# Loads and scalings of units 5 to 9 moved earlier in the first two groups of a fused attention and feed-forward kernel

## The chip, the cores and the metric

The kernel runs on one core of a Trainium2 chip. The metric is the device time of one execution in microseconds (us). A core has a matrix engine (TensorE, PE in the profile; its weight loads are PEld), a vector engine (VectorE, DVE), a scalar engine (ScalarE, ACT), GpSimd (POOL) and SyncE (SP). SyncE here only issues DMAs; GpSimd issues those of the weights and of v, and computes as well.

## The reference

Two stages: linear attention with decay over 4 batches, 8 heads, 768 positions and head size 64, and a bilinear feed-forward layer over the 3072 resulting rows of 512.

```python
for b in range(nb):                      # blocks of positions
    intra = (q_b @ k_b.T * Dmask) @ v_b  # Dmask: lam**(i-j) for i >= j, else 0
    inter = (q_b * lam_pow) @ kv_state
    out[b] = intra + inter
    kv_state = lam_block * kv_state + (k_b * rev_pow).T @ v_b
x = out as 3072 rows of 512
y = ((x @ w_a) * (x @ w_b)) @ w_out      # w_a, w_b: 512 x 1536, w_out: 1536 x 512
```

## The kernel before, in words

The 3072 rows are 24 units of 128 rows (6 to a batch). `GROUPS = (4, 2, 4, 4, 4, 4, 2)` cuts them into feed-forward groups: units 0 to 3, then 4 and 5 (group 1), then 6 to 9 (group 2), and so on. While the feed-forward layer of one group runs, the attention of the next group's units is put between its matmuls.

Per unit, in `prep_k` (L263, step "P" of the plan): k is scaled by a power of lam on VectorE for units 4 to 9 and on GpSimd from 10 on (`make_ks`, L249; the instruction is at L244), q is scaled on GpSimd (`make_qs`), from unit 6 on a transposing DMA is issued on SyncE (L269), then `pump` issues more loads of q and k, and outside it `make_vb` (L257) loads v by a DMA that GpSimd issues. Units 4 and 5 are transposed on TensorE instead (step "T", L275). Step "S" computes the scores of a unit (L294) and masks them (two VectorE instructions, L311). Step "V" updates the state by matmuls (L358) and copies it out on VectorE (L391). Step "O2" takes two units, computes their attention output (L328), copies it to `xT` on ScalarE (L351), and, with the last unit of a group, makes the four sums of x (`sums`, L480 to L483) that the group's products need.

`pump` (L160) walks a list `pending`. An entry ("q", u) or ("k", u) issues a 256 KB load on SyncE's queue, into one of four buffers each for q and k (`load_x`, L123), unless u is 3 or more ahead of the units already prepared; then it stops until the next step P. An entry "after" is a gate: a copy of one element out of a weight tile, which SyncE can issue only once that part of the weights has landed; all later loads stand behind it. In order the list before has: gate on part 3 of w_b, unit 4, gate on part 0 of w_out, unit 5, gate on part 3 of w_out, unit 6, gate on part 5 of w_out, unit 7 and on. The first call of `pump` is just ahead of group 0.

`PLAN` (L43) gives for each group pairs of a slot and a step; `hook(slot)` emits the steps of a slot between matmuls. Group 0 (`ffn`, L621) has slots 0 to 11 after the feed-forward products and 12 to 35, each after two output matmuls (L612). Groups 1 to 6 use `ffn_seven` (L488), a product with seven instead of eight block products. `step(i, n)` is product n of column block i, called (i, n) below. For group 1, i is 0 to 2, and the products run in the order

```
(0,1) (0,5) (0,2) (0,6) (0,3) (1,1) (0,7) (1,5) (1,2) (1,6) (0,4) (1,3) (2,1) (1,7) (2,5) (2,2) (2,6) (1,4) (2,3) (2,7)
```

with the slots of `hook` after (0,1): 0, (0,6): 1, (0,7): 2, (1,6): 3, (1,7): 4, (2,6): 5, (2,7): 6 and 7, and then 11; then come eight output matmuls, the last product (2,4), and the slots from 12 on.

Each product is eight matmuls (L502) into one of seven PSUM banks that are handed out in turn. ScalarE copies three of a block's partial results out (L517). VectorE then forms c11 (product 2, L536), c12 (product 3, L547), c22 (product 7, L553) and the second half of `ab` (product 4, L556), and GpSimd the first half (L549). Product 4 adds to the bank that c22 reads. `SUM_ON_VEC` (L42) lists the blocks whose c11 is made on VectorE; for the others ScalarE makes one more copy and GpSimd adds (L539).

The pool `wst` has 13 buffers of 4 KB per partition, used by the first loads of q and k (six of them, free once units 0 to 3 are scaled), the weight sums, the x sums, `s12` and kept outputs.

Of the kernel before, what the change touches and what calls it, by code (L numbers as in the profile page):

```python
# [16 lines left out]
F32 = mybir.dt.float32  # L17
# [5 lines left out]
def _bc(ap, dims):  # L23
# [15 lines left out]


S_GROUPS = (1, 2, 3, 4, 5, 6)
SUM_ON_VEC = {1: (0, 1, 2), 2: (0, 1, 2, 3, 5), 3: (1, 3, 5), 4: (1, 3, 5), 5: (1, 2, 4, 5), 6: (0, 1, 2)}  # L42
PLAN = {  # L43
    0: [(0, "V", 3), (1, "TW", 0), (3, "TW", 1), (5, "TW", 2), (7, "TW", 3), (11, "TW", 4),
        (15, "P", 4), (18, "TW", 5), (19, "T", 4), (20, "P", 5), (22, "S", 4), (25, "T", 5), (26, "V", 4),
        (27, "P", 6), (28, "S", 5), (31, "O2", (4, 5)), (33, "P", 7)],
    1: [(2, "P", 8), (4, "P", 9), (6, "S", 6), (7, "V", 6), (7, "S", 7), (11, "O2", (6, 7)),
        (12, "S", 8), (12, "V", 8), (13, "S", 9), (13, "P", 10), (14, "O2", (8, 9)), (15, "P", 11)],
    2: [(1, "P", 12), (4, "P", 13), (7, "P", 14), (11, "S", 10), (11, "S", 11), (12, "P", 15),
        (14, "P", 16), (17, "P", 17)],  # L50
# [11 lines left out]
def kernel(  # L62
# [11 lines left out]
    nc = tc.nc  # L74
    B, H, S, D = q.shape
# [5 lines left out]
    NU = B * NB  # L81
# [6 lines left out]
    wst_pool = ctx.enter_context(tc.tile_pool(name="wst", bufs=13))  # L88
    ld_pool = ctx.enter_context(tc.tile_pool(name="ld", bufs=4))
# [31 lines left out]
    raw = {}  # L121

    def load_x(w, u):  # L123
        b, nb = divmod(u, NB)
        t = ld_pool.tile([128, H, D], F32, name=w + "f", tag=w + "f", bufs=4)
        nc.sync.dma_start(out=t, in_={"q": qr, "k": kr}[w][b, nb])
        raw[u, w] = t

    wa_sb = singles.tile([128, KS, d_ff], BF16, name="wa_sb")
    wb_sb = singles.tile([128, KS, d_ff], BF16, name="wb_sb")  # L130
    wo_sb = singles.tile([128, FC, d_model], BF16, name="wo_sb")
# [4 lines left out]
    w_off = [sum(W_CHUNKS[:i]) for i in range(len(W_CHUNKS) + 1)]  # L136
# [7 lines left out]
    def load_w(kind, c):  # L144
        if kind == "o":
            nc.gpsimd.dma_start(out=wo_sb[:, 2 * c:2 * c + 2, :], in_=wo_r[:, 2 * c:2 * c + 2, :])
        else:
# [1 line left out]
                                in_=w_part(wa_r if kind == "a" else wb_r, c))  # L149

    n0 = GROUPS[0]
    pending = [("after", ("b", 3)), ("q", n0), ("k", n0), ("after", ("o", 0)), ("q", n0 + 1), ("k", n0 + 1),
               ("after", ("o", 3)), ("q", n0 + 2), ("k", n0 + 2), ("after", ("o", 5))]
    for u in range(n0 + 3, NU):
        pending += [("q", u), ("k", u)]
    landed = singles.tile([1, 16], BF16, name="landed")
    q_here = singles.tile([128, 1], F32, name="q_here")
    used = {"u": 0, "gates": 0}

    def pump():  # L160
        while pending:
            kind, c = pending[0]
            if kind == "after":
                i = used["gates"] = used["gates"] + 1
                nc.sync.dma_start(out=landed[:, i:i + 1],
                                  in_=wo_sb[0:1, 2 * c[1] + 1, 0:1] if c[0] == "o" else
                                  wb_sb[0:1, 3, w_off[c[1]]:w_off[c[1]] + 1])
            elif c >= used["u"] + 3:
                return
            else:  # L170
                load_x(kind, c)
            pending.pop(0)
# [15 lines left out]
    for w, src in (("q", q), ("k", k)):  # L188
# [3 lines left out]
        for c in range(0, HP, n_c):  # L192
            t = wst_pool.tile([128, 1024], F32, name=w + "4", tag="wst")[:, :n_c * 512]
            t = t.rearrange("p (c b x) -> p c b x", c=n_c, b=2)
# [68 lines left out]
    def prep_k(u):  # L263
        make_ks(u, "dve" if u < n0 + 6 else "pool")
        make_qs(u, "pool")
        used["u"] = u + 1
        if u in DMA_T:
            qkT = qkT_pool.tile([128, 2, HP, 128], BF16, name="qkT", tag="qkT")
            nc.sync.dma_start_transpose(  # L269
                out=qkT[:].rearrange("p j hp i -> p (j hp) i"),  # L270
                in_=U[u]["qk"][:].rearrange("p j h d -> p (j h d)"))
            U[u]["qT"], U[u]["kT"] = qkT[:, 0], qkT[:, 1]
        pump()
# [214 lines left out]
    def ffn_seven(g, u0, n, xT, hook, last):  # L488
# [31 lines left out]
        def step(i, n):  # L520
# [10 lines left out]
            elif n == 2:  # L531
                p, pb = bank_of("m_p")
                product(i, p, w_of(wa_sb, 2, i), x12, True)
                d["c11"] = a_pool.tile([128, nf, h], BF16, name="c11", tag="a")
                if i in SUM_ON_VEC[g]:
                    nc.vector.tensor_add(d["c11"], d["s12"][:, 0], p)  # L536
# [254 lines left out]
    bank["held"].clear()  # L791
    used["u"] = n0
    pump()

    for g, n in enumerate(GROUPS):
# [62 lines left out]
```

## Time and profile before

| | |
|---|---|
| four runs | 225.86 to 227.85 us, median 226.77 |
| the profiled execution | 226.27 us; span from first to last instruction 224.6 us |
| TensorE busy | 214.8 us, 96% of the span; granted clock 0.991 on average |
| VectorE, ScalarE, GpSimd busy | 148.8, 100.2, 121.0 us |
| DMA queue of SyncE (q1) | 23.53 MB, 47.3% of 16 engines' span |
| DMA queue of GpSimd (q0) | 7.87 MB, 38.4% |
| loads of q and of k, 20 each | 256 KB, median 4.7 and 5.5 us from issue to landing |

Times inside the execution are counted from its first instruction. Group 0's feed-forward products begin at 17.45 us and its output matmuls at 38.41. Group 1 begins at 52.86, its last output matmuls end near 76.9, where group 2 begins. "Busy" of TensorE includes time in which it runs at a lower clock. A wait is named by the instruction that waited and the one that released it; the chain of waits follows the execution back from its end through those releases.

### The profile page before, as it was taken

The numbers are of one execution on the slowest core, as the hardware profiler recorded it, in microseconds if no ns is written. First come the engines' busy times: TensorE is split into PE (matmuls) and PEld (weight loads), VectorE is DVE, ScalarE is ACT, GpSimd is POOL, SyncE is SP. The second block draws the span as 40 slices with busy tenths as digits, with TensorE's granted clock in tenths as the row PEclk, the third lists the DMA queues.
The fourth block names the chain that finished last, engine by engine and source line by source line (L and its number), as shares of the span: only waits on it lengthen the run. The fifth ranks groups of instructions, "written<-read, shape, count | busy, mean of one in ns | idle before, by whom it ended". The sixth has DMA issues, their size and how long they took to land.

```text
span 224.6 us, 5362 instructions
## 1 busy us (share of the span) xinstructions
PE 214.8 (96%) x2171; PEld 148.2 (66%) x2171; DVE 148.8 (66%) x254; ACT 100.2 (45%) x179; POOL 121.0 (54%) x134
## 2 busy tenths in 40 slices
PE   7799999989959999999999999999999999999994
PEld 2476444447935688855588855688854688745973
DVE  0992995674994789793877773678873687820760
ACT  2685232118601565523366523566423556333622
POOL 6879541160898339997059994069920146400230
PEclk9999999999997999999999999999999999999999
DMA  4999999999999995999985959509511200012102
GB/s 125 299 182 193 204 197 181 195 219 165 208 217 186 240 175 71 234 332 228 207 227 66 169 146 231 141 0 74 70 50 47 93 4 0 0 50 93 50 3 93
DMA packets 98608, 31.81 MB, mean 142 GB/s; under 512 B 86552, under 2 KB 95640, under 8 KB 98584
## 3 DMA queue, kind: packets, MB, share of 16 engines
q1 hardware_dynamic: 66392, 23.53, 47.3%
q0 software_dynamic: 31904, 7.87, 38.4%
q8 instruction: 17, 0.28, 0.5%
q10 hardware_dynamic: 288, 0.07, 0.1%
q14 instruction: 7, 0.06, 0.1%
HBM read 28.32 MB, written 6.29 MB: 154 GB/s over the span
## 4 chain that ended last, share of the span: by engine, by line
PE 73%; DMA 13%; DVE 4%; POOL 3%; ACT 2%; SPq 2%; issue 1%; ACTq 0%
PE op L612 24%; PE m_q L502 23%; PE m_r L502 12%; PE m_p L502 6%; DMA kf<-in_k_dram 6%; DMA wo_sb<-in_moe_w_out_dram 5%; PE o_ps L328 4%; DMA k<-in_k_dram 3%; PE kq L294 2%; DVE m L311 2%; POOL wa_sb L148 1%; POOL wb_sb L148 1%; SPq L196 1%; PE kvd L358 1%; ACT o_kept L603 1%
## 5 line engine op out<-in xcount | busy, mean ns | idle before, releaser
L612 PE MATMUL op<-wo_sb,ab 128*128 128x512 bf16 (+2 forms) x312 | 69.0, 367 | 0.0
L549 POOL TENSOR_TENSOR ab<-c,c 128x512 bf16<-128x512 bf16 x30 | 34.8, 1164 | 43.2 <-DVE c L547 42.3
L502 PEld LDWEIGHTS <-tw 128*128 128x128 bf16 x576 | 49.1, 98 | 6.4 <-issue 0.3
L612 PEld LDWEIGHTS <-ab 128*128 128x128 bf16 x312 | 28.0, 99 | 27.4 <-issue 1.1
L502 PE MATMUL m_q<-xs,tw 128*128 128x256 bf16 (+1 forms) x288 | 36.1, 255 | 0.2 <-ACT s L517 0.2
L311 DVE TENSOR_TENSOR m<-kq,lotri 128x512 bf16<-128x512 f32 x47 | 29.8, 683 | 4.2 <-PE kq L294 3.8
L607 ACT COPY o_sb<-op 128x512 f32<-128x512 f32 (+2 forms) x20 | 10.9, 543 | 43.5 <-PE op L612 43.5
L556 DVE TENSOR_TENSOR ab<-c,m_q 128x512 bf16<-128x512 f32 x30 | 20.6, 687 | 13.0 <-PE m_q L502 11.2
L244 POOL TENSOR_TENSOR qk<-qf,lp_q 128x512 bf16<-128x512 f32 x20 | 21.8, 1089 | 13.3 <-DMA qf<-in_q_dram 13.3
L539 POOL TENSOR_TENSOR c<-s 128x512 bf16<-128x512 f32 x9 | 11.5, 1274 | 30.8 <-ACT s L517 30.7
L502 PEld LDWEIGHTS <-wa_sb 128*128 128x128 bf16 x288 | 24.5, 98 | 3.1
L517 ACT COPY s<-m_q 128x512 f32<-128x512 f32 x30 | 17.6, 588 | 15.0 <-PE m_q L502 14.9
L547 DVE TENSOR_TENSOR c<-u,m_r 128x512 f32<-128x512 f32 x30 | 20.4, 681 | 5.5 <-ACT u L517 5.5
L260 POOL DMA_DIRECT2D vb<-in_v_dram x24 | 22.4, 935 | 1.4 <-DMA wb_sb<-in_moe_w_b_dram 1.4
L536 DVE TENSOR_TENSOR c<-s,m_p 128x512 bf16<-128x512 f32 x21 | 14.4, 686 | 12.6 <-PE m_p L502 11.2
L553 DVE TENSOR_TENSOR c<-s,m_q 128x512 f32<-128x512 f32 x30 | 20.5, 685 | 0.5
L517 ACT COPY s<-m_r 128x512 f32<-128x512 f32 x30 | 17.7, 590 | 7.1 <-PE m_r L502 7.1
L517 ACT COPY u<-m_q 128x512 f32<-128x512 f32 x30 | 17.8, 593 | 5.9 <-PE m_q L502 5.9
L351 ACT CAST xT<-o_ps 128x512 bf16<-128x512 f32 x22 | 12.0, 588 | 17.4 <-PE o_ps L328 17.2
L502 PE MATMUL m_q<-xT,wa_sb 128*128 128x256 bf16 (+1 forms) x144 | 18.1, 255 | 0.0
L502 PE MATMUL m_q<-xT,tw 128*128 128x256 bf16 (+1 forms) x144 | 18.1, 255 | 0.0
L502 PE MATMUL m_r<-xs,tw 128*128 128x256 bf16 (+1 forms) x144 | 18.1, 255 | 0.0
(81 smaller groups left out, 264.2 us busy)
## 6 DMA issues: line engine op xcount, KB each, us to landing
qf<-in_q_dram SPq DMA_DIRECT2D x20, 256.0 KB, 4.7
kf<-in_k_dram SPq DMA_DIRECT2D x20, 256.0 KB, 5.5
out_dram<-o_sb SPq DMA_DIRECT2D x17, 256.0 KB, 2.0
vb<-in_v_dram POOLq DMA_DIRECT2D x24, 128.0 KB, 4.6
wa_sb<-in_moe_w_a_dram POOLq DMA_DIRECT2D x6, 256.0 KB, 6.2
wb_sb<-in_moe_w_b_dram POOLq DMA_DIRECT2D x6, 256.0 KB, 7.5
wo_sb<-in_moe_w_out_dram POOLq DMA_DIRECT2D x6, 256.0 KB, 12.1
out_dram<-o_kept SPq DMA_DIRECT2D x6, 256.0 KB, 3.5
```

The source lines that it names most:

```text
L244: eng_of(eng).tensor_mul(dst.rearrange("p (c b) d -> p b c d", b=2), x[:].rearrange("p (b c) d -> p b c d", b=2), lp.rearrange("p (b c) o ...
L260: nc.gpsimd.dma_start(out=vb, in_=vr[b, nb])
L311: nc.vector.tensor_mul(m, kq[i], lotri_bc)
L351: nc.scalar.copy(dst, src)
L502: nc.tensor.matmul(ps[:, f, :], lhsT=w(k, f), rhs=x[:, k, :], start=(first and f == 0 and k == 0), stop=True, skip_group_check=True)
L517: nc.scalar.copy(t, ps)
L536: nc.vector.tensor_add(d["c11"], d["s12"][:, 0], p)
L547: nc.vector.tensor_add(c12, d["u2"], d["r"])
L549: nc.gpsimd.tensor_mul(ab[:, nf * i:nf * i + nf, 0:h], d["c11"], c12)
L553: nc.vector.tensor_add(d["c22"], d["s5"], d["q"])
L556: nc.vector.tensor_mul(ab[:, nf * i:nf * i + nf, h:2 * h], d["c22"], d["q"])
L612: nc.tensor.matmul(op[:, lo:hi], lhsT=ab[:, f, t * 128:(t + 1) * 128], rhs=wo_sb[:, f, lo:hi], start=(f == 0), stop=(f == FC - 1))
```

## The change

Three things change.

- The list `pending` has two gates instead of four: on part 3 of w_b ahead of unit 4 (as before) and on part 5 of w_b ahead of unit 6. The bound on how far loads may run ahead is raised at the start, so that the first call of `pump` issues q and k of units 4 to 9.
- q and k of units 8 and 9 go into halves of one `wst` tile per unit instead of the four buffers, which units 4 to 7 hold.
- The plan: in group 0, T of unit 5 goes from slot 25 to 24, V of 4 from 26 to 25, S of 5 from 28 to 27, P of 6 from 27 to 28 (so behind S of 5), P of 7 from 33 to 30 (ahead of O2 of 4 and 5 with the x sums), and P of 8 from group 1 into slot 35 (behind O2). In group 1, P of 9 goes from slot 4 to 0, S of 6 from 6 to 4, V of 6 from 7 to 5 and S of 7 from 7 to 6. In group 1, c11 of block 1 is made by ScalarE and GpSimd instead of VectorE.

```diff
-SUM_ON_VEC = {1: (0, 1, 2), 2: (0, 1, 2, 3, 5), 3: (1, 3, 5), 4: (1, 3, 5), 5: (1, 2, 4, 5), 6: (0, 1, 2)}
+SUM_ON_VEC = {1: (0, 2), 2: (0, 1, 2, 3, 5), 3: (1, 3, 5), 4: (1, 3, 5), 5: (1, 2, 4, 5), 6: (0, 1, 2)}
 PLAN = {
     0: [(0, "V", 3), (1, "TW", 0), (3, "TW", 1), (5, "TW", 2), (7, "TW", 3), (11, "TW", 4),
-        (15, "P", 4), (18, "TW", 5), (19, "T", 4), (20, "P", 5), (22, "S", 4), (25, "T", 5), (26, "V", 4),
-        (27, "P", 6), (28, "S", 5), (31, "O2", (4, 5)), (33, "P", 7)],
-    1: [(2, "P", 8), (4, "P", 9), (6, "S", 6), (7, "V", 6), (7, "S", 7), (11, "O2", (6, 7)),
+        (15, "P", 4), (18, "TW", 5), (19, "T", 4), (20, "P", 5), (22, "S", 4), (24, "T", 5), (25, "V", 4),
+        (27, "S", 5), (28, "P", 6), (30, "P", 7), (31, "O2", (4, 5)), (35, "P", 8)],
+    1: [(0, "P", 9), (4, "S", 6), (5, "V", 6), (6, "S", 7), (11, "O2", (6, 7)),
         (12, "S", 8), (12, "V", 8), (13, "S", 9), (13, "P", 10), (14, "O2", (8, 9)), (15, "P", 11)],
...
     def load_x(w, u):
         b, nb = divmod(u, NB)
-        t = ld_pool.tile([128, H, D], F32, name=w + "f", tag=w + "f", bufs=4)
+        if u in (n0 + 4, n0 + 5):
+            if (u, "kq") not in raw:
+                raw[u, "kq"] = wst_pool.tile([128, 2, H, D], F32, name="qkf", tag="wst")
+            t = raw[u, "kq"][:, "qk".index(w)]
+        else:
+            t = ld_pool.tile([128, H, D], F32, name=w + "f", tag=w + "f", bufs=4)
         nc.sync.dma_start(out=t, in_={"q": qr, "k": kr}[w][b, nb])
...
     n0 = GROUPS[0]
-    pending = [("after", ("b", 3)), ("q", n0), ("k", n0), ("after", ("o", 0)), ("q", n0 + 1), ("k", n0 + 1),
-               ("after", ("o", 3)), ("q", n0 + 2), ("k", n0 + 2), ("after", ("o", 5))]
-    for u in range(n0 + 3, NU):
+    pending = [("after", 3)]
+    for u in range(n0, NU):
+        if u == n0 + 2:
+            pending.append(("after", 5))
         pending += [("q", u), ("k", u)]
...
-    used = {"u": 0, "gates": 0}
+    used = {"u": 0}
...
             if kind == "after":
-                i = used["gates"] = used["gates"] + 1
-                nc.sync.dma_start(out=landed[:, i:i + 1],
-                                  in_=wo_sb[0:1, 2 * c[1] + 1, 0:1] if c[0] == "o" else
-                                  wb_sb[0:1, 3, w_off[c[1]]:w_off[c[1]] + 1])
-            elif c >= used["u"] + 3:
+                nc.sync.dma_start(out=landed[:, c:c + 1], in_=wb_sb[0:1, 3, w_off[c]:w_off[c] + 1])
+            elif c >= max(used["u"] + 3, n0 + 6):
                 return
```

## The prediction

> **What bounds the kernel now.** I read the page first: TensorE is busy 96% of the span, so the change can earn only what TensorE loses. The waits of TensorE say where that is:
>
> ```profile
> PE o_ps L328 <- DVE st L391: 2.0, 1, 2.0
> ...
> PE tps L280 <- DVE qk L244: 0.9, 1, 0.9
> PE kq L294 <- DVE ab L556: 0.6, 1, 0.6
> ...
> PE m_q L502 <- ACT s L517: 0.2, 1, 0.2
> ```
>
> (Columns: waiting line, who ended the wait, us in all, times, longest.) Three of them end on VectorE, and all lie between 45 and 67 us. The chain of waits in that stretch:
>
> ```profile
> 33.16 12.70 DMA kf<-in_k_dram
> 45.86 0.02 issue
> 45.88 0.70 DVE qk L244
> 46.59 0.05 issue
> 46.63 0.40 PE tps L280 x4
> ...
> 62.45 0.68 DVE ab L556
> 63.12 0.06 DVE c L547
> 63.18 0.46 issue
> 63.64 0.68 DVE c L553
> 64.32 1.20 DVE m L311 x2
> 65.52 0.60 DVE st L391
> 66.11 0.61 DVE m L311
> 66.72 0.04 issue
> 66.77 1.02 PE o_ps L328 x12
> 67.79 0.21 PE kvd L380 x8
> 68.00 2.90 PE op L612 x8
> ```
>
> The reader should see two places. At 46 us TensorE waits for k of unit 5 to land and be scaled. From 62.45 to 66.72 the chain lies on VectorE: it is behind, and the masks and the state of units 6 and 7 come last. Then eight 512-column matmuls take 2.90 us; elsewhere in the chain two take 0.43, so eight should be 1.73. The stretch by half microseconds says why (columns: PE, PEld, DVE, ACT, POOL busy, granted clock, DMA share, GB/s):
>
> ```profile
> 64.50:65.00 0.50, 0.00 (x0) 0.00 (x0) 0.50 (x2) 0.00 (x0) 0.50 (x2) 1.00 1.26 283
> 65.00:65.50 0.50, 0.00 (x0) 0.00 (x0) 0.50 (x2) 0.00 (x0) 0.50 (x1) 1.00 1.27 265
> ...
> 66.50:67.00 0.50, 0.44 (x10) 0.33 (x12) 0.50 (x2) 0.00 (x0) 0.50 (x2) 0.73 1.42 228
> 67.00:67.50 0.50, 0.50 (x12) 0.35 (x9) 0.31 (x1) 0.28 (x1) 0.50 (x1) 0.50 1.36 163
> ...
> 69.50:70.00 0.50, 0.50 (x2) 0.15 (x1) 0.00 (x0) 0.00 (x0) 0.50 (x2) 0.50 1.46 244
> ```
>
> After the idle stretch the granted clock halves from about 66.7 to 70.1. From the last product of group 1 (ends 62.4) to 70.9 TensorE does about 3.6 us of work in 8.5: some 4.9 us are lost here, 1.7 of them to the clock. After that no wait over 0.2 us is listed, so what is won here stays won.
>
> VectorE is behind because it scales k of units 7, 8 and 9 at 53.05 (0.69 us), 57.22 (1.11) and 60.65 (1.28), while it stood idle 1.91 us before 52.12, 0.83 before 54.57 and 0.59 before 55.85. That is what the moved steps address.
>
> **The change, part by part.**
>
> *Gates and issue order.* Two of four gate copies go (0.60 and 0.88 us on SyncE; at 44.21 one delays q of unit 7), and k, q of unit 5 are issued at about 27.5 instead of 32.73 and 33.16. Does k of unit 5 land earlier? I counted the SyncE queue's 256-byte packets in the trace; q or k of one unit is 1,024. From 29 to 43 us they flow without a gap, one for one with those of the weights and v (161 against 161 in the microsecond from 31, 373 against 379 from 34). The queue is in order and already full, so issuing earlier buys nothing before packet 4,096 (k of unit 5), at 44.1. I take zero; if it does come earlier, at most the 0.91 us wait goes. SyncE itself stands in such issues (2.94 us at 33.16, 3.41 at 40.70, each until an older load has landed), so by the same pace it gets past k of 9 at about 50.4; the transposing DMA of 6, whose k is scaled at 50.8, finds it free.
>
> *Step T of unit 5 one slot earlier.* Its second half still waits until 46.63, but two matmuls that ran before the wait now run behind it: +0.43 us. Their cover is that wait, and it is lost. P, S and V of units 4 and 5 shift inside the same absolute times. Group 1 starts 0.43 later, at 53.29.
>
> *Units 6 and 7.* Step P issues, in order: k scaling on VectorE, q scaling on GpSimd (1.03), a transposing DMA on SyncE, two loads if some come free (now only from P of unit 7 on, as units up to 9 are issued), and v on GpSimd (0.94). k of 6 and 7 are now scaled behind the masks of unit 5 at about 50.1 and 50.7 and before the sums L480 to L483, in the 1.91 us that VectorE stood idle. k of 7 is complete at packet 8,192; before, that was at 49.0, and with the time from last packet to use of k of 5 (44.1 to 45.88, 1.8) it is usable at 50.8. Cover: the sums cannot start before ScalarE's copy ends at about 52.5, so 1 us of lateness is free; more delays group 1 one for one.
>
> *Units 8 and 9.* Their scalings come between the sums and the first product sums of group 1, and k of 9 stands ahead of c11 of product block 0 (L536), so whatever that load is late VectorE is late. This is the new wait. Behind it queue c11, c12, c22, and TensorE's product (0,4) at 57.75 + 0.43 = 58.2 overwrites the bank that c22 reads. When does k of 9 land? Low end: 12,288 packets at the best rate seen alone (1,000 per us) from 4,096 at 44.1: 52.3, usable at 53.6 to 54.1. High end: as before the change, packet 13,312 at 57.1, usable at 58.8. Between: 6,144 packets at 950 take us to 50.6 (k of 8), then v of 6, 7 and 8 share the engines. Where both queues had work they moved some 520 packets per us each (475 against 564 at 65); 2,048 more take 4.0 us: 54.6, usable near 56.4 to 56.8. I take 56.6. Then k of 9 takes 0.69, c11 and c12 0.60 each, c22 0.69: 59.1, and product (0,4) is held 0.9 us.
>
> The tiles of the other pool are as large as the old ones together and the packets stay 256 bytes; I cost them at nothing, since six buffers used by the first loads come free early. The transposing DMAs of 6 and 7 now run behind k of 9 (from about 54.6, 2 to 2.5 us each by the dips at 53.5 and 58.2): units 6 and 7 are ready near 58.5 and 61; they are needed at about 61 and 64.4.
>
> *S6, V6, S7 spread.* S6 now stands behind product (1,7), V6 behind (2,6), S7 behind (2,7). Product (1,7) ended at 59.55; with 0.43 and 0.9 it ends at 60.9. From there VectorE has in order c22 of block 1, two masks of 6, c11 of block 2, the state of 6, ab, c12, c22, two masks of 7: ten operations at 0.60 start to start, the last 0.69 long, so the last mask ends 0.05 + 9 x 0.60 + 0.69 = 6.1 later, at 67.0. Before it was 67.31. TensorE needs only some 4 us for its part, so VectorE still sets this end, and much of the gain is eaten by the wait for k of 9.
>
> *One sum moves.* c11 of block 1 leaves VectorE (0.69 us, counted above) for a copy on ScalarE (0.58) and an addition on GpSimd (1.27). ScalarE is half idle there; GpSimd waits 5.82 us before 56.62, so it is covered; uncovered, it would delay the first early output matmuls by about 1.
>
> *The clock.* TensorE's idle time is broken up: a hold of 0.9 near 58.5, then pieces of 0.7, 0.8 and 0.4 between 64.4 and 67.0 with work between. From 63.3 to 66.7 it is busy some 1.9 us, against 1.25 before. Bounds: the drop stays (the tail after the last mask 3.6 us, as 67.31 to 70.91) or goes (0.4 for the rest of o and kv, 1.73 for eight matmuls: 2.15). I take the second, since no other stretch of this trace after the start shows a drop, also not around the 0.9 us wait at 46.
>
> The Trainium skill ("TensorE: Matmul & The Clock Gate", Part 1) says that the clock halves after an idle window of about 3.4 us of a free-running clock, and its advice is to avoid idle gaps over some 3 us. By that advice even the present gaps (longest 1.96 us) should not drop it; the trace shows they do, so the measurement decides and the threshold is not known. By the rule no drop follows and the sum is the one below; by the trace alone a shorter gap could still drop it, and the sum is 1.4 higher.
>
> **Sum.** 67.0 + 2.15 = 69.15 against 70.9: 1.7 us less. The profiled execution took 226.27 us (span 224.6 and 1.7 around it), so 224.6; the median of the four runs is 0.5 higher, so I predict 225.1.
>
> **Rivals.**
> 1. *Clock drops anyway*: 67.0 + 3.6 = 70.6, gain 0.3: 226.5. For it: VectorE is still the last; against it: shorter gaps.
> 2. *All loads in time*: k of 9 usable by 55.7, product (0,4) not held. (1,7) ends at 60.0, the last mask at 66.1, clock kept: 68.25, gain 2.65: 224.1. For it: 950 to 1,000 packets per us when alone; against it: v of 6 to 8.
> 3. *k of 9 late, slower*: VectorE stands at the load with c11, c12, c22 behind it. Each us beyond 55.7 is a us at the end (last mask at landing + 2.5 - 58.2 + 60.0 + 6.1 = landing + 10.4). With the clock kept it breaks even at 58.3 (58.3 + 10.4 + 2.15 = 70.9), with the drop at 56.9 (56.9 + 10.4 + 3.6). At 59.8, one us beyond the former landing: +1.5 with the clock kept, +2.9 with a drop, 229.7. For it: long idle at 58 invites the drop, and v competes; against it: k of 9 now stands ahead of two transposes.
> 4. *The load order does nothing*: k of 9 lands at 58.8 as before; with the clock kept +0.5, 227.3.
>
> **How the numbers follow.** Chances: forecast 0.42, rival 1 0.18, rival 2 0.19, rival 3 0.13, rival 4 0.08. The forecast's own range is 224.2 to 226. About 1% (2.3 us) is what a measurement can tell from no change: faster than 224.5 needs rival 2 or the favourable third of the forecast: 0.28; slower than 229.0 needs rival 3: 0.14; within 0.58. Range 223.3 to 228.4.
>
> **What would show it.** Right: TensorE's wait for k of 5 grows to some 1.3; a VectorE wait for kf of unit 9 near 54 to 57; a state wait at o_ps under 1 us; clock 1.00 from 64 to 71; products of group 2 some 1.7 us earlier. Wrong: k of 5 scaled before 45; k of 9 without a wait, or past 58; a clock of 0.50 after 64; waits for the transposes of 6 or 7.

## The result, and the profile after

The changed kernel takes 225.2 us (median of 38 runs, 224.1 to 227.74); beside it the kernel before took 226.43 (59 runs). The ratio is 0.9947, 95% interval 0.9932 to 0.9962: about 1.2 us faster. The profiled execution after took 226.56 us, span 224.9, so the profile shown here is of one of the longer runs; why some are longer is the main finding. Runs more than 1.5% above the fastest of their kernel count in the medians and not in the ratios (one run of the last experiment, 246.41 us at a mean granted clock of 0.854, is the farthest).

The waits of TensorE after the change, columns as before:

```profile
PE m_q L505 <- DVE c L556: 1.4, 1, 1.4
...
PE tps L283 <- DVE qk L247: 1.2, 1, 1.2
PE o_ps L331 <- DVE m L314: 0.8, 2, 0.7
PE o_ps L331 <- DVE c L550: 0.5, 1, 0.5
```

(Lines are three higher: L314 are masks, L556 is c22, L550 c12, L247 scalings.) The wait for the state of unit 6 is gone. In its place stand waits for c12 and the masks (1.3 together), and a new one of 1.4 at product (0,4). The wait at step T grew from 0.9 to 1.2. VectorE's wait for k of unit 9, foreseen, is there:

```profile
56.95 0.70 DVE L247 TENSOR_TENSOR qk<-qkf,lp_k 128x512 bf16<-128x512 f32 x1 [2.01 <-DMA qkf<-in_k_dram]
```

The chain of waits after:

```profile
51.00 5.93 DMA qkf<-in_k_dram
56.93 0.02 issue
56.95 0.03 DVE qk L247
...
57.58 0.68 DVE c L539
58.26 0.60 DVE c L550
58.85 0.61 DVE c L556
59.46 0.04 issue
59.51 0.61 PE m_q L505 x8
...
65.68 0.68 DVE c L556
66.36 1.21 DVE m L314 x2
67.57 0.04 issue
67.61 0.30 PE o_ps L331 x4
67.92 0.13 PE kvd L383 x4
68.04 3.47 PE op L615 x8
```

It now runs through the load of k of unit 9, which lands at 56.93 and holds c11, c12 and c22 one behind the other; product (0,4) starts at 59.51. The last mask ends at 67.56 (before: 67.31). Then the eight matmuls take 3.47 us, since the clock dropped here too. The half microseconds (columns as before):

```profile
67.50:68.00 0.50, 0.39 (x13) 0.34 (x13) 0.06 (x1) 0.49 (x2) 0.50 (x2) 1.00 1.23 269
68.00:68.50 0.50, 0.50 (x5) 0.23 (x3) 0.42 (x1) 0.50 (x1) 0.50 (x2) 0.57 4.44 49
...
71.00:71.50 0.50, 0.50 (x4) 0.23 (x3) 0.00 (x0) 0.00 (x0) 0.50 (x1) 0.52 1.37 241
```

By this profile nothing was won: group 2 starts at 77.54, before at 76.89. The gain shows when the runs are sorted by the mean granted clock that each of them recorded. No run lies between 0.992 and 0.997; the profiles at 0.997 or more show no drop, those at 0.992 or less show one.

| kernel | runs | without drop, median us | with drop, median us |
|---|---|---|---|
| before | 64 | 3 (224.88, 225.56, 227.31) | 61: 226.56 |
| changed | 46 | 34: 225.1 | 12: 226.85 |

With a drop the changed kernel is no faster than before. Without one it is 1.75 us faster than with one. What changed is how often the drop comes: in 61 of 64 runs before, in 12 of 46 after. The difference of the two shares, 0.69, times 1.75 us is 1.2 us, as much as the gain. (The rows count every run that recorded a clock, those beside the experiments too, and one more set of the changed kernel, called "copy" below. On the one chip where both were recorded side by side, 18 of 20 runs before had the drop and 1 of 7 of the copy.)

### The profile page after: what moved, and what is told of

Same layout as the page of the kernel before. It is cut to its first block, busy times and chain, and to the rows that moved or that the text cites. A ratio compares the mean times of both kernels' runs of the same rounds, so it can differ in the third digit from the quotient of the medians.

```text
span 224.9 us, 5363 instructions
## 1 busy us (share of the span) xinstructions
PE 215.6 (96%) x2171; PEld 148.2 (66%) x2171; DVE 148.1 (66%) x253; ACT 100.7 (45%) x180; POOL 121.3 (54%) x135
## 4 chain that ended last, share of the span: by engine, by line
PE 69%; SPq 13%; DMA 8%; DVE 4%; POOL 1%; issue 1%; ACT 1%; ACTq 0%; DVEq 0%
PE op L615 23%; PE m_q L505 22%; PE m_r L505 11%; SPq L131 10%; PE m_p L505 5%; PE o_ps L331 3%; DMA wb_sb<-in_moe_w_b_dram 3%; DMA qkf<-in_k_dram 3%; DMA k<-in_k_dram 2%; PE kq L297 2%; SPq L170 2%; DVE m L314 1%; SPq L199 1%; DVE c L556 1%; PE kvd L361 1%
## 5 line engine op out<-in xcount | busy, mean ns | idle before, releaser
L615 PEld LDWEIGHTS <-ab 128*128 128x128 bf16 x312 | 28.0, 99 | 27.5 <-issue 1.3
L314 DVE TENSOR_TENSOR m<-kq,lotri 128x512 bf16<-128x512 f32 x47 | 29.8, 684 | 4.7 <-PE kq L297 4.3
L542 POOL TENSOR_TENSOR c<-s 128x512 bf16<-128x512 f32 x10 | 12.7, 1272 | 30.8 <-ACT s L520 30.8
L247 POOL TENSOR_TENSOR qk<-qf,lp_q 128x512 bf16<-128x512 f32 x18 | 18.8, 1042 | 13.2 <-DMA qf<-in_q_dram 13.2
L550 DVE TENSOR_TENSOR c<-u,m_r 128x512 f32<-128x512 f32 x30 | 20.4, 682 | 5.0 <-ACT u L520 5.0
L539 DVE TENSOR_TENSOR c<-s,m_p 128x512 bf16<-128x512 f32 x20 | 13.7, 686 | 11.5 <-PE m_p L505 11.5
L556 DVE TENSOR_TENSOR c<-s,m_q 128x512 f32<-128x512 f32 x30 | 20.6, 685 | 0.5
```

The lines of the kernel that those rows point to most:

```text
L247: eng_of(eng).tensor_mul(dst.rearrange("p (c b) d -> p b c d", b=2), x[:].rearrange("p (b c) d -> p b c d", b=2), lp.rearrange("p (b c) o ...
L314: nc.vector.tensor_mul(m, kq[i], lotri_bc)
L550: nc.vector.tensor_add(c12, d["u2"], d["r"])
L556: nc.vector.tensor_add(d["c22"], d["s5"], d["q"])
L615: nc.tensor.matmul(op[:, lo:hi], lhsT=ab[:, f, t * 128:(t + 1) * 128], rhs=wo_sb[:, f, lo:hi], start=(f == 0), stop=(f == FC - 1))
```

## The experiments

Theory A is the prediction's: VectorE is late at O2 of units 6 and 7, and k of unit 9 holds it. Theory H came after the sorting by clock: the whole gain is that the drop comes less often. The rivals give the gain to one part alone. Each ratio is to runs of the kernel before on the same chip. Of each changed line only the part that differs is shown.

**One sum moved, alone.**

```diff
-SUM_ON_VEC = {1: (0, 1, 2),      # kernel before
+SUM_ON_VEC = {1: (0, 2),
```

> The kernel before with one edit: c11 of block 1 of group 1 made by ScalarE and GpSimd instead of VectorE. Theory A (VectorE is behind from 55.9 to 67.3 us, so each of its operations removed there ends the last mask 0.60 us earlier): 226.4 - 0.6 = 225.8 us, last mask of units 6 and 7 near 66.7 us. Rival B (this move carries the gain of the change): 225.2 us. Rival C (it changes nothing, TensorE waits elsewhere): 226.4 us.

Measured: 226.91 us, ratio 1.0009 (0.9985 to 1.0033). No gain, so rival B falls, theory A's 0.6 us did not come either, and rival C's time holds, though not for its reason: VectorE itself is no earlier. Its rows in this run:

```profile
58.96 0.69 DVE L556 TENSOR_TENSOR ab<-c,m_q 128x512 bf16<-128x512 f32 x1
59.56 0.68 DVE L547 TENSOR_TENSOR c<-u,m_r 128x512 f32<-128x512 f32 x1
60.30 0.69 DVE L553 TENSOR_TENSOR c<-s,m_q 128x512 f32<-128x512 f32 x1
60.91 1.65 DVE L244 TENSOR_TENSOR qk<-kf,lp_k 128x512 bf16<-128x512 f32 x1
```

and GpSimd's:

```profile
60.71 1.29 POOL L539 TENSOR_TENSOR c<-s 128x512 bf16<-128x512 f32 x1
62.07 1.50 POOL L549 TENSOR_TENSOR ab<-c,c 128x512 bf16<-128x512 bf16 x1
```

The sum that left VectorE runs on GpSimd at the same time as VectorE's scaling of k of 9, and that scaling takes 1.65 us instead of 1.28. From the scaling of k of 8 to that of k of 9 it is 3.13 us here and 3.43 before, so half of the 0.60 is saved; from there to c11 of block 2 it is 1.57 and 1.20, and it is lost again. From product (0,4) to the last mask it is 9.63 us here and 9.56 before.

**S6, V6, S7 spread, alone.**

```diff
-(6, "S", 6), (7, "V", 6), (7, "S", 7),   # kernel before, group 1
+(4, "S", 6), (5, "V", 6), (6, "S", 7),
```

> The kernel before with one edit: S of 6, V of 6, S of 7 in slots 4, 5, 6 of group 1. Theory A: VectorE has the same number of operations in the stretch, so its last mask still ends near 67.3 us; the wait for the state of unit 6 goes, waits for masks take its place, and the time falls only where the shorter gaps keep the clock up: 226.4 us with the drop of the clock, about 224.8 without. Rival B (the order S, V, S carries the gain by itself): last mask near 66 us and 225.2 us also in runs with a drop.

Measured: 226.82 us, ratio 0.9987 (0.9951 to 1.0023); 3 of 12 runs without a drop (median 224.97). Theory A holds, rival B falls: from the start of group 1 to the end of the last mask it is 14.45 us in both profiles. TensorE's waits at o_ps are now 1.0, 0.9 and 0.7 in place of one of 2.0, and the drop still came in 9 of 12 runs.

**P of unit 9 behind c22 of block 0.**

```diff
-    1: [(0, "P", 9), (4, "S", 6),            # changed kernel
+    1: [(2, "P", 9), (4, "S", 6),
```

> The changed kernel with step P of unit 9 in slot 2 of group 1, behind c22 of block 0, instead of slot 0. Theory A (k of 9 lands at 57 us and holds c11, c12 and c22 of block 0 and with them product (0,4) for 1.4 us): VectorE's wait for k of 9 falls below 0.3 us, product (0,4) is not held, the last mask ends 1.3 us earlier, near 66.2 us: 223.5 us without a clock drop, 225.4 with one, median near 223.8. Rival D (the hold is harmless, VectorE's sum of work sets the end): 225.2 us, as the changed kernel.

Measured: 223.89 us, ratio 0.9909 (0.9875 to 0.9944). Theory A holds, rival D falls. Without a drop it is 223.88 (5 runs), with one 225.43 (2), each some 1.3 below the changed kernel. VectorE's rows of this run:

```profile
56.66 0.69 DVE L556 TENSOR_TENSOR c<-s,m_q 128x512 f32<-128x512 f32 x1
57.26 1.11 DVE L247 TENSOR_TENSOR qk<-qkf,lp_k 128x512 bf16<-128x512 f32 x1
...
64.59 1.28 DVE L314 TENSOR_TENSOR m<-kq,lotri 128x512 bf16<-128x512 f32 x2
```

c22 of block 0 no longer waits for k of 9, which has landed when its turn comes; product (0,4) starts at 57.80 and the last mask ends at 65.87.

**The old loads under the new plan.** `pending`, `pump` and `load_x` as before the change, all else as changed.

```diff
-    pending = [("after", 3)]
...
+    pending = [("after", ("b", 3)), ("q", n0), ("k", n0), ("after", ("o", 0)), ("q", n0 + 1), ("k", n0 + 1),
+               ("after", ("o", 3)), ("q", n0 + 2), ("k", n0 + 2), ("after", ("o", 5))]
```

> The changed kernel's plan and sums with the loads of before (four gates, four buffers each, three units ahead). Theory A: q and k of 9 are again issued behind the transposing DMA of 6, k of 9 is usable near 59.5 us instead of 57, VectorE stands at it ahead of c11, and the end moves by the same 2.5 us: 227.4 us or more. Rival E (the order of the loads is worth nothing, the plan is all): 225.2 us.

Measured: 229.52 us, ratio 1.0099 (1.0061 to 1.0136). Rival E falls: the plan needs the earlier loads. VectorE's row and TensorE's wait:

```profile
58.50 0.69 DVE L244 TENSOR_TENSOR qk<-kf,lp_k 128x512 bf16<-128x512 f32 x1 [4.09 <-DMA kf<-in_k_dram]
```

```profile
PE m_q L502 <- DVE c L553: 2.5, 1, 2.5
```

k of 9 is used at 58.50, 1.5 later than in the changed kernel (2.5 were expected), and product (0,4) is held 2.5 us. 8 of 9 runs have a drop; in four the mean clock is 0.985 or less, as a second drop at this longer hold would give, but no profile here shows one.

**v of 6 to 9 issued later.**

```diff
-                    if us > n0 + 1:          # changed kernel, hook
+                    if us > n0 + 5:
                         make_vb(us)
+                elif name == "B":
+                    make_vb(us)
...
-    1: [(0, "P", 9), (4, "S", 6),
+    1: [(0, "P", 9), (0, "B", 6), (0, "B", 7), (1, "B", 8), (2, "B", 9), (4, "S", 6),
```

> The changed kernel with the loads of v of units 6 to 9 issued in slots 0 to 2 of group 1, behind the scaling of q of 9, instead of each behind its own step P. Theory A (v of 6 to 8 shares the DMA engines with k of 8 and 9 and so makes k of 9 late): VectorE's wait for k of 9 falls from 2.0 us to below 0.5, product (0,4) is held less than 0.3 us, and the time falls as with P of 9 in slot 2: about 223.9 us in runs with the clock at 0.998 or more, 225.5 in runs with a drop. Rival F (the SyncE queue alone sets the landing of k of 9): the wait stays at 2 us and the time at 224.9 and 226.7.

Measured: 225.3 us, ratio 0.9934 (0.9912 to 0.9956). The mechanism is shown, the time only half: VectorE's wait for k of 9 falls from 2.01 to 0.73 us and product (0,4) is not held, so v's share of the engines did delay it (rival F falls). Runs with a drop are 1.2 below the changed kernel (225.64), runs without one only 0.4 (224.68, 5 runs), and 7 of 12 have a drop. Two of VectorE's rows:

```profile
54.88 0.71 DVE L247 TENSOR_TENSOR qk<-qkf,lp_k 128x512 bf16<-128x512 f32 x1 [0.73 <-DMA qkf<-in_k_dram]
...
73.66 1.03 DVE L483 TENSOR_TENSOR xs<-xT 128x512 bf16<-128x512 bf16 x1 [1.38 <-ACT xT L354]
```

From the start of group 1 to that of group 2 the profile takes 21.23 us, 0.99 less than the copy without a drop (22.22). Most of it is lost again at once: two of the sums of x for group 2, 0.43 and 0.42 us in the profile after, take 1.03 and 1.15 beside two of GpSimd's scalings, and the first five products of group 2 take 2.96 us instead of 2.25.

**O2 of 6 and 7 behind the eight output matmuls and (2,4).**

```diff
-    (6, "S", 7), (11, "O2", (6, 7)),         # changed kernel
+    (6, "S", 7), (12, "O2", (6, 7)),
```

> The changed kernel with O2 of units 6 and 7 in slot 12 of group 1, behind the eight first output matmuls and product (2,4), instead of slot 11. Theory A (TensorE stands at O2 because VectorE is still at c12, c22 and the masks; 2.2 us of other matmuls are ready): the waits at o_ps fall below 0.3 us, the clock stays up in nearly all runs, 224.85 - 1.6 = 223.2 us and few runs over 225. Rival G (VectorE's end is all that counts, the matmuls then wait for ab and c22 in the same way): 225.2 us with the same share of drops.

Measured: 224.16 us, ratio 0.9882 (0.9858 to 0.9906), 6 of 6 runs without a drop. Theory A holds for the waits and the clock: no wait at o_ps is left in the profile. Against runs of the changed kernel without a drop it is 0.9 us less, not 1.6. The hold at (0,4) is still 1.2 us here and no run has a drop; with v later there is no hold and 7 of 12 have one. So the stand at O2 brings the drop, not the hold.

**Both edits together, and T of 5 back as well.**

> Both edits: step P of unit 9 in slot 2 and O2 of 6 and 7 in slot 12 of group 1. Theory A (two separate losses, the hold by k of 9 and the stand at O2): they add up, 223.9 - 1.5 = 222.4 us, clock 0.997 or more in nearly all runs. Rival: the second edit only covers what the first one removes, 223.2 us.

> As the last one, with T of unit 5 and V of 4 back in slots 25 and 26 of group 0. Theory A (T one slot earlier puts two matmuls behind the wait for k of 5): 0.4 us less, 222.0 us, and the wait for the scaling of k of 5 falls from 1.1 to 0.8 us. Rival (VectorE sets the end, so what TensorE wins in group 0 it waits out in group 1): 222.4 us.

Measured: 223.52 us, ratio 0.9882 (0.9839 to 0.9926), with both; 224.38, ratio 0.9885 (0.9854 to 0.9916), with T back. The first two losses add up only in part: without a drop it is 223.34 us, against 223.88 and 224.16 for each edit alone, nearer to the rival's 223.2 than to 222.4. In the profile group 1 to group 2 takes 20.60 us, 1.62 less than in the copy, and the first five products of group 2 then take 3.25 us instead of 2.25. The third edit brings nothing, and both of its numbers were missed; in that run TensorE next waits for the transposing DMAs:

```profile
PE kq L297 <- DMA qkT<-qk: 1.2, 2, 0.8
```

**The kernel before with O2 later, and nothing of the change.**

```diff
-    (7, "S", 7), (11, "O2", (6, 7)),         # kernel before
+    (7, "S", 7), (12, "O2", (6, 7)),
```

> The kernel before, nothing of the change, with O2 of units 6 and 7 in slot 12 of group 1 instead of 11. Theory H (what the changed kernel gains is only that the clock drops in fewer of its runs; before, 40 of 44 runs with a known clock show the drop, and runs of equal clock take equal time before and after): the eight matmuls fill the gap, the drop goes in nearly all runs, and the kernel before falls below the changed one, 222.9 to 224 us. Rival A (VectorE's shorter chain is part of the gain, the clock the rest): a drop remains in many runs, 225.4 us or more.

Measured: 224.2 us, ratio 0.9894 (0.9866 to 0.9922), 5 of 6 runs without a drop (223.99). This is 0.2 above the range of theory H and well under rival A's 225.4: moving one step does more than the whole change. (The 40 of 44 runs in the expectation are 43 of 44 by the recorded clocks.) TensorE's rows of this run:

```profile
63.62 0.40 PE L294 MATMUL kq<-qkT 64*128 64x128 bf16 x8
64.18 1.67 PE L612 MATMUL op<-wo_sb,ab 128*128 128x512 bf16 x7 [0.16 <-issue]
65.69 0.61 PE L502 MATMUL m_q<-xT,tw 128*128 128x128 bf16 x8
66.23 0.31 PE L328 MATMUL o_ps<-qkT,st 64*64 64x128 bf16 x8
```

The matmuls that stood behind O2 now run while VectorE catches up, and at full clock: from their start to product (2,4) it is 65.69 - 64.18 = 1.51 us, before 70.74 - 67.93 = 2.81.

**T of 5 back, alone.**

```diff
-(24, "T", 5), (25, "V", 4)                   # changed kernel
+(25, "T", 5), (26, "V", 4)
```

> The changed kernel with T of unit 5 and V of 4 back in slots 25 and 26 of group 0. Group 1 starts 0.43 us earlier after the wait for k of 5. Theory A (product (0,4) waits for k of 9 anyway, so the 0.43 us are waited out there): no change, 224.85 us with the clock up, 226.75 with a drop. Rival: 0.43 us less in both.

Measured: 225.34 us, ratio 0.9955 (0.9929 to 0.998); 10 of 12 runs without a drop, 225.1, the same as the changed kernel. Theory A's time holds: what TensorE wins at T does not show at the end. From T's second half to group 1 this profile takes 6.32 us, the copy 6.66; product (0,4) starts at 59.84 and 59.77, since in both it waits for k of 9.

**The changed kernel once more.**

> The changed kernel once more, for a profile and more clocks. If the profile shows no drop, group 1 to group 2 takes 24.47 - 1.7 = 22.8 us in place of the 24.47 of the profile with a drop, with the same hold of 1.4 us at product (0,4). 225.2 us, about 7 runs in 10 without a drop.

Measured: 225.42 us, ratio 0.9965 (0.9935 to 0.9994); 6 of 7 runs without a drop. Its profile has none. From the start of group 1 to that of group 2 it takes 22.22 us against 24.47, 2.25 less and not 1.7: the clock gives 1.6 of it, and a hold at (0,4) of 0.8 us instead of the 1.4 expected gives 0.6. First TensorE's rows after the last mask, then the 3.4 us up to the end of the waiting:

```profile
68.47 1.67 PE L615 MATMUL op<-wo_sb,ab 128*128 128x512 bf16 x7 [0.16 <-POOL qk L247]
69.98 0.61 PE L505 MATMUL m_q<-xT,tw 128*128 128x128 bf16 x8
```

```profile
64.90:68.30 3.40, 2.03 (x43) 1.31 (x42) 2.93 (x5) 0.67 (x2) 2.19 (x3) 1.00 1.23 276
```

and the same stretch of the profile after, with a drop, and of before:

```profile
64.60:68.00 3.40, 2.03 (x45) 1.29 (x43) 2.96 (x5) 0.63 (x2) 2.16 (x3) 1.00 1.14 227
```

```profile
63.30:66.70 3.40, 1.44 (x31) 0.86 (x28) 3.40 (x7) 0.00 (x0) 3.31 (x4) 1.00 1.48 237
```

TensorE is busy 2.03 of 3.40 us in both executions of the changed kernel, and the clock drops in one and not in the other; before it was 1.44.

The clock records show why nearly the same gap can end either way. In all 14 profiles the stretches of full and of half clock between two changes last a whole number of times 3.413 us (18, 1 and 45 times in the profile before). So a grid of 3.413 us can be laid over each trace from its first change. On it the drop after the change follows the stretch 64.65 to 68.07, with TensorE busy 2.04 us; in the copy the grid cuts the same gap at 64.16 and 67.58, busy 2.23, and no drop follows. An estimate from these traces: of all positions of the grid, the share that leaves TensorE 2.1 us or less in some stretch near this gap is 1.0 before, 0.4 after the change, and 0 with O2 later; measured were drops in 61 of 64, 12 of 46 and 0 of 6 runs. The estimate is rough: with P of 9 in slot 2 it is 0 as well, and 2 of 7 runs had a drop. Nor is busy time the whole rule: 2.03 us from 57.83 to 61.24 in the profile after, and 1.53 from 67.67 to 71.09 in the last experiment, were followed by no drop. What else counts no run tests.

**v later and O2 later.**

> The changed kernel with the loads of v of 6 to 9 in slots 0 to 2 of group 1 and O2 of 6 and 7 in slot 12. Theory A (v's share of the DMA engines and the stand at O2 are two losses): 224.16 - 1.2 = 222.9 us, no drops, group 1 to group 2 near 20.2 us. Rival: the second edit covers what the first removes, 224.2 us.

Measured: 224.53 us, ratio 0.989 (0.9859 to 0.992). Theory A's sum fails, and the rival's 224.2 is near: the time goes to S of 9, which waits 1.78 us for its transposing DMA:

```profile
70.75 0.40 PE L297 MATMUL kq<-qkT 64*128 64x128 bf16 x8 [1.78 <-DMA qkT<-qk]
```

## Why the prediction was right

It foresaw 225.1, with 1.7 us of gain, of which 0.3 from VectorE's chain and 1.4 from the clock; measured were 225.2 and 1.2. That the two times agree within 0.1 is partly luck. The sum gave 224.6 from the profiled execution, and 0.5 was added because the median of four runs lay that far above it; the median of 59 runs lies 0.16 above. A gain 0.5 too large met an offset 0.34 too large.

- *The clock*: right for most runs, and it was all of the gain. The tail after the last mask was put at 3.6 us with a drop and 2.15 without; measured from the last mask's end to the last product 71.31 - 67.56 = 3.75 and 69.98 - 67.83 = 2.15. What it had as two cases of one execution are two kinds of runs: 34 of 46 without. So one of its own signs of being wrong, a clock of 0.50 after 64, stands in the profile after, and group 2 starts 0.65 later there and 0.77 earlier in the copy (76.12), not 1.7. TensorE's 1.25 us from 63.3 to 66.7 before are 1.44 by the view.
- *VectorE's chain*: mis-sized. k of 9 was to be used at 56.6; it was at 56.95 and, in the copy, 57.23. Two errors cancel here: its last packet started at 55.97, not at 54.6, and it was used 1.0 later, not 1.8 to 2.2. The hold at (0,4) was put at 0.9 and measured 1.4 and 0.8. From the end of product (1,7), 61.3 (0.45 behind its start, as the prediction counts it; 60.9 was foreseen), to the last mask, 67.56, it is 6.3 us; 6.1 was foreseen. So the 0.3 of gain became 0.25 of loss (67.56 against 67.31), and rival 1 (drop anyway) came out at 226.85 in place of 226.5, above the kernel before with a drop.
- *T one slot earlier*: +0.43, as foreseen. From T's second half to group 1 it is 6.23 us before, 6.66 after. But it does not reach the end (T back alone: no change).
- *Loads*: k of 5 lands no earlier (used at 45.88 before, 45.66, 46.49 and 46.78 in profiles with the new loads; it varies from run to run), as foreseen. Its issue did not move to 27.5: SyncE stood 5.06 us in the issue of q of 5 and came to k of 5 at 31.91; it got past k of 9 at 52.2, not 50.4, and the transposes were still in time. k of 9 lands earlier by leaving the place behind the transposing DMA (used at 56.95, and at 58.50 with the old loads), so rival 4 fell.
- *The sum moved*: counted as 0.60 us of VectorE saved; alone it saved nothing.
- *The transposes of 6 and 7* were in time in the changed kernel; those of 9 are the next limit once the other waits are gone (waits of 0.8 to 1.8 us in three experiments).
- The Trainium skill ("TensorE: Matmul & The Clock Gate", Part 1) speaks of a free-running window and of cold phases that differ from run to run. The runs agree: nearly equal gaps drop the clock in 12 runs of 46, and the drops start on a grid of 3.413 us that lies differently in each trace. Its advice to avoid gaps over some 3 us is too lax here, since the longest gap in group 1 is 2.0 us before the change and 1.4 after.

No part of the change brings the rarer drop alone: runs without one are 1 of 12 with the sum, 3 of 12 with the spread steps, 1 of 9 with all but the loads. The lowest median is that of the version with P of 9 in slot 2 and O2 of 6 and 7 in slot 12, 223.52 us; by the ratio to the kernel before it cannot be told from O2 later alone (0.9882 both), nor from the kernel before with O2 later (0.9894).

## What to carry to other kernels

Where TensorE waits in pieces, record the clock of every run and sort by it before reading any gain: one profile shows one of two kinds of runs, and here the profile after looked like no gain at all. Where one engine is late, look first for work of the waiting engine that is ready and can go ahead of the wait; here that took one slot number and won more than a rearranged order of loads. An operation on a load that is moved to the head of an engine's work must find the load landed, or everything behind it waits; two slots later VectorE did not wait for it.

## What was not expected of the hardware

- The drop is worth 1.75 us of median and lasts 3.41 us (66.7 to 70.1 and 68.1 to 71.5 in the two profiles). TensorE was busy 1.44 us of the 3.41 ahead of it in the profile before, where 61 of 64 runs drop, and 2.04 in the profile after, where 12 of 46 do.
- VectorE's scaling of k takes 0.69 us while GpSimd computes nothing (at 53.05 before). Started while GpSimd's half of `ab` or its addition of c11 runs, it ends 0.55 us behind that operation's end: 58.33 and 57.78, 61.93 and 61.38 (1.11 and 1.28 us, before), 62.56 and 62.00 (1.65 us, with the sum alone). In these three rows it looks held until GpSimd is done, so work given to GpSimd was not free for VectorE.
- A load on SyncE's queue can hold SyncE for long when older ones are open: the issue of q of 5 took 5.06 us in the profile after, without a loss, as k of 5 was used at 45.66 and before at 45.88.
